# A row copy set behind other work, and two weight loads cut in halves, in a sparse attention and ELU MLP kernel

## The chip, the cores and the metric

The kernel runs on one core of one Trainium2 chip. The metric is device time in microseconds of one execution, smaller is better; where several runs were taken, their median counts. Five engines matter: TensorE (PE, matmuls; PEld is its weight loading), VectorE (DVE), ScalarE (ACT), GpSimd (POOL, which here issues the loads from HBM) and SyncE (SP, which issues the stores and the DMA transposes). Each works through its own list of instructions in order, and they wait for one another by semaphores.

## What is computed

Causal attention over 8 batches, 8 heads, 576 positions and 64 features per head, in which four heads see the last 32 positions ("local") and four see the earlier positions of the same remainder modulo 32 ("strided"); the heads of a token, side by side, are a row of `x`, which goes through two matmuls with an ELU between.

```python
rel = pos[:, None] - pos[None, :]
mask_local = (rel >= 0) & (rel < stride)
mask_strided = (rel >= 0) & (pos[None, :] % stride == pos[:, None] % stride)
...
attn = np.exp(scores)
attn = attn / (np.sum(attn, axis=-1, keepdims=True) + 1e-09)
return np.matmul(attn, v).astype(np.float32)
...
h = x @ w_in
g = np.where(h > 0.0, h, alpha * (np.exp(np.minimum(h, 0.0)) - 1.0))
return (g @ w_out).astype(np.float32)
```

`x` has 4608 rows of 512, `w_in` is 512 x 2048, `w_out` 2048 x 512. Inputs and output are float32; the kernel computes in bf16 with float32 sums.

## The kernel before

The order of all work is written out by hand, in the string `ORDER` (lines 35 to 145). Each word of it is one step; a loop at the end (lines 703 to 705) splits a word at its dots and calls the function of its first letter with the rest. Every engine gets its instructions in the order of these words, so a word's place counts against the words of the same engine and those it waits for.

The steps of attention, for a batch `b` and a pair of heads (`s` strided or `l` local, with y = 0 or 1; `0l1` is batch 0, local, y = 1) and half u:

- `D.what.b` issues loads on POOL (line 267). `D.vl` loads the rows of local v (line 260), `D.wi3.0` a quarter of `w_in` (512 columns, all four groups of 128 rows, line 275), `D.wo..` a quarter of `w_out`. Words with one number more (`D.kl.0.1`) load a part. Loads share eight semaphores in turn.
- `T` transposes q or k on PE (lines 404 to 415) and `c` (DVE) or `C` (ACT) copies the result. From batch 2 on, `X` does it by a DMA transpose on SP (line 604).
- `S.key.u.banks` computes scores into two PSUM banks (L456); `e` takes their exp on ACT (L463), into one of two buffers; `m` multiplies by the mask on DVE (L470 strided, L476 local).
- `O.key.u.banks` multiplies by ones, for the sums, and by v (L483 and L492 strided, L499 and L504 local in batches 0 and 1; L519 and L526 later); `n` takes the logarithm of the sums and `r` the exp of minus that, on ACT (L554, L559); `x` multiplies on DVE and writes a part of `xT` (L584).
- `V.b` copies, on DVE, the last 32 rows of each block of local v to the first rows of the next block (L588). The load of v must have landed, and L504 reads what V wrote. In batches 0 and 1 only; later a load does it (L262). `W` copies strided v (L591).
- `F.mk` makes the local mask on POOL (two selects, L349 and L352), `F.ml` spreads it on DVE (L357, L359).

The steps of the MLP, for a chunk of 512 tokens and a tile m of 128 of the 2048 columns:

- `a` does the first two of four matmuls of a tile, over the strided heads' features (row groups 2 and 3 of `w_in`), `b` the other two (groups 0 and 1, the local heads); `L` does all four (L611). The last number is the PSUM bank.
- `h` takes the exp (ACT, L619); `i` on DVE (L628) or `j` on ACT (L626) clamps it; `g` takes the maximum with h on DVE (L637, L639) and so frees the bank.
- `Z` does a quarter of the second matmul (L645), `o` (ACT) or `q` (DVE) copies the result (L651), `t` stores it (L663).

`w.bank.n...` are matmuls on zeros (L390) of n columns each, whose results are not used; they keep PE going at the start. Buffers come from small pools (two for e, five for masked scores, three for logarithms, line 169 on).

For `D.wi`, the function for loads already takes a third number: without one it loads all four row groups, with 0 the groups 2 and 3, with 1 the groups 0 and 1 (line 274).

Of the kernel before, what the change touches and what calls it, by code (L numbers as in the profile page):

```python
# [15 lines left out]
S = 576  # L16
# [30 lines left out]
h.0.15 b.0.12 h.0.14 i.0.15 b.0.0 h.0.12 b.0.13 i.0.14 g.0.15 h.0.0 a.0.3.7 D.vs.1 a.0.11.3 j.0.12
g.0.14 a.0.2.1 h.0.1 i.0.0 b.0.2 g.0.12 b.0.3 h.0.2 g.0.0 b.0.11 h.0.3 a.0.8.6 i.0.2 D.ql.1 h.0.11 i.0.1
a.0.6.4 g.0.2 h.0.13 a.0.5.0 b.0.8 g.0.1 a.0.4.1 D.kl.1 h.0.8 i.0.3 b.0.4 g.0.3 b.0.5 h.0.4 T.1s1.q.2
a.0.7.7 j.0.13 i.0.4 b.0.6 C.1s1.q g.0.4 b.0.7 D.vl.1 h.0.5 g.0.13 Z.0.1.0.2 h.0.6 i.0.5 Z.0.0.0.5 g.0.5  # L50
h.0.7 D.qs.2 j.0.6 i.0.8 a.0.9.1 i.0.7 a.0.10.0 g.0.8 b.0.9 g.0.6 j.0.11 b.0.10 g.0.7 h.0.9 T.1s1.k.6
Z.0.3.0.4 D.ks.2 h.0.10 g.0.11 j.0.10 Z.0.3.1.4 i.0.9 c.1s1.k g.0.10 Z.0.0.1.5 g.0.9 Z.0.1.1.2 D.kl.2
T.1s0.q.3 T.1s0.k.7 C.1s0.q Z.0.1.2.2 c.1s0.k S.1s0.1.01 S.1s1.0.67 Z.0.0.2.5 e.1s1.0 e.1s0.1 Z.0.0.3.5
m.1s0.1 m.1s1.0 S.1s1.1.01 S.1s0.0.67 e.1s1.1 Z.0.1.3.2 e.1s0.0 m.1s1.1 O.1s0.1.31 o.0.1 m.1s0.0
O.1s1.0.07 T.1l1.q.6 n.1s0.1 n.1s1.0 Z.0.3.2.4 c.1l1.q r.1s0.1 q.0.0 D.vs.2 r.1s1.0 O.1s1.1.76 x.1s1.0
T.1l1.k.5 n.1s1.1 O.1s0.0.21 c.1l1.k T.1l0.q.0 n.1s0.0 T.1l0.k.6 x.1s0.1 D.ql.2 Z.0.3.3.4 C.1l0.k
c.1l0.q r.1s1.1 V.1 S.1l0.1.01 r.1s0.0 S.1l0.0.56 x.1s1.1 Z.0.2.0.3 e.1l0.0 q.0.3 X.qs.2 e.1l0.1 m.1l0.0
S.1l1.1.56 e.1l1.1 m.1l0.1 S.1l1.0.01 O.1l0.0.74 e.1l1.0 X.ks.2 m.1l1.1 O.1l0.1.65 x.1s0.0 Z.0.2.1.3
n.1l0.0 n.1l0.1 m.1l1.0 r.1l0.0 O.1l1.1.54 t.0.3 r.1l0.1 x.1l0.0 O.1l1.0.21 n.1l1.1 x.1l0.1 Z.0.2.2.3
n.1l1.0 r.1l1.1 t.0.0 r.1l1.0 Z.0.2.3.3 x.1l1.1 x.1l1.0 X.kl.2 W.2 L.1.12.7 L.1.1.6 h.1.12 i.1.12  # L60
L.1.6.5 h.1.1 g.1.12 o.0.2 D.qs.3 L.1.0.4 i.1.1 h.1.6 g.1.1 L.1.4.7 h.1.0 i.1.6 g.1.6 L.1.5.6 X.ql.2
h.1.4 D.ks.3 i.1.0 j.1.4 L.1.3.5 g.1.0 D.vs.3 h.1.5 t.0.1 g.1.4 L.1.2.4 D.vl.2 h.1.3 i.1.5 i.1.3
S.2s1.0.01 S.2s1.1.23 h.1.2 g.1.3 L.1.10.7 e.2s1.0 g.1.5 D.ql.3 e.2s1.1 L.1.15.5 i.1.2 h.1.10 g.1.2
L.1.7.6 h.1.15 m.2s1.1 i.1.15 S.2s0.0.01 S.2s0.1.23 h.1.7 X.qs.3 g.1.15 L.1.13.4 e.2s0.1 i.1.10 j.1.7
L.1.9.5 m.2s0.1 g.1.10 L.1.8.3 g.1.7 h.1.9 e.2s0.0 i.1.9 L.1.14.7 X.ks.3 h.1.13 g.1.9 L.1.11.6 h.1.8
i.1.13 h.1.14 i.1.8 Z.1.2.0.5 t.0.2 g.1.13 h.1.11 j.1.14 g.1.8 O.2s1.1.01 Z.1.3.0.4 j.1.11 D.kl.4
n.2s1.1 g.1.11 Z.1.2.1.5 g.1.14 r.2s1.1 O.2s0.1.23 m.2s1.0 Z.1.3.1.4 n.2s0.1 x.2s1.1 O.2s1.0.67 r.2s0.1
Z.1.2.2.5 n.2s1.0 x.2s0.1 Z.1.3.2.4 r.2s1.0 m.2s0.0 O.2s0.0.01 x.2s1.0 Z.1.3.3.4 n.2s0.0 r.2s0.0
S.2l0.0.23 S.2l0.1.67 Z.1.2.3.5 o.1.3 x.2s0.0 e.2l0.1 Z.1.0.0.4 W.3 o.1.2 m.2l0.1 e.2l0.0 S.2l1.0.01
S.2l1.1.67 Z.1.1.0.5 e.2l1.1 m.2l0.0 e.2l1.0 m.2l1.1 O.2l0.0.23 D.kl.3 Z.1.0.1.4 n.2l0.0 m.2l1.0  # L70
O.2l1.1.01 r.2l0.0 O.2l1.0.67 Z.1.1.1.5 n.2l1.0 x.2l0.0 n.2l1.1 Z.1.1.2.5 r.2l1.0 O.2l0.1.23 Z.1.0.2.4
r.2l1.1 x.2l1.0 D.vs.4 n.2l0.1 x.2l1.1 Z.1.0.3.4 r.2l0.1 D.ks.4 Z.1.1.3.5 x.2l0.1 D.qs.4 S.3s0.0.01
S.3s0.1.67 q.1.1 L.2.5.3 e.3s0.0 D.vl.3 q.1.0 e.3s0.1 L.2.14.5 h.2.5 m.3s0.1 L.2.3.4 i.2.5 h.2.14 D.ql.4
g.2.5 X.kl.3 L.2.11.7 h.2.3 i.2.14 g.2.14 O.3s0.1.01 h.2.11 L.2.0.6 X.ql.3 i.2.3 m.3s0.0 n.3s0.1 L.2.4.5
i.2.11 r.3s0.1 g.2.3 t.1.3 O.3s0.0.23 h.2.0 g.2.11 L.2.8.4 h.2.4 x.3s0.1 L.2.2.7 n.3s0.0 i.2.4 X.qs.4
i.2.0 h.2.8 L.2.9.1 g.2.4 r.3s0.0 i.2.8 L.2.7.5 g.2.0 h.2.9 X.ks.4 h.2.2 g.2.8 L.2.10.0 h.2.7 i.2.2
x.3s0.0 L.2.13.6 X.kl.4 j.2.7 j.2.9 g.2.2 L.2.6.4 h.2.13 g.2.7 t.1.0 L.2.1.7 j.2.13 g.2.9 h.2.6 g.2.13
L.2.15.5 t.1.2 h.2.1 i.2.6 j.2.1 L.2.12.6 g.2.6 h.2.15 g.2.1 S.3s1.0.12 S.3s1.1.34 h.2.10 i.2.15
Z.2.1.0.7 e.3s1.1 i.2.10 e.3s1.0 m.3s1.1 Z.2.1.1.7 g.2.10 h.2.12 m.3s1.0 Z.2.0.0.4 i.2.12 g.2.15
S.3l0.0.01 S.3l0.1.23 g.2.12 Z.2.0.1.4 e.3l0.1 e.3l0.0 X.ql.4 m.3l0.1 S.3l1.0.23 S.3l1.1.56 Z.2.1.2.7  # L80
m.3l0.0 e.3l1.0 e.3l1.1 m.3l1.0 t.1.1 O.3s1.1.01 Z.2.1.3.7 n.3s1.1 m.3l1.1 O.3l1.1.23 r.3s1.1 O.3s1.0.56
Z.2.0.2.4 n.3l1.1 x.3s1.1 n.3s1.0 Z.2.0.3.4 q.2.1 r.3l1.1 O.3l1.0.01 t.2.1 r.3s1.0 Z.2.3.0.7 x.3l1.1
n.3l1.0 x.3s1.0 Z.2.3.1.7 r.3l1.0 S.4s1.0.23 S.4s1.1.56 x.3l1.0 Z.2.3.2.7 e.4s1.0 e.4s1.1 W.4 O.3l0.0.01
Z.2.3.3.7 q.2.0 n.3l0.0 D.vs.5 O.3l0.1.23 r.3l0.0 t.2.0 D.kl.5 Z.2.2.0.6 n.3l0.1 x.3l0.0 Z.2.2.1.6
r.3l0.1 m.4s1.1 O.4s1.1.01 x.3l0.1 Z.2.2.2.6 n.4s1.1 q.2.3 D.qs.5 L.3.2.5 r.4s1.1 m.4s1.0 D.ks.5 x.4s1.1
L.3.11.7 h.3.2 D.vl.4 i.3.2 S.4l0.0.01 S.4l0.1.23 h.3.11 g.3.2 L.3.14.4 e.4l0.1 i.3.11 e.4l0.0 L.3.7.5
m.4l0.1 g.3.11 S.4s0.0.01 S.4s0.1.23 m.4l0.0 h.3.7 Z.2.2.3.6 e.4s0.1 i.3.7 e.4s0.0 g.3.7 L.3.4.7 h.3.14
m.4s0.1 L.3.5.5 h.3.4 i.3.14 m.4s0.0 O.4s0.1.01 g.3.14 h.3.5 L.3.8.3 n.4s0.1 i.3.5 L.3.0.4 g.3.5 r.4s0.1
i.3.4 L.3.1.2 o.2.2 X.ks.5 x.4s0.1 h.3.0 O.4s0.0.56 g.3.4 h.3.8 L.3.3.1 i.3.0 X.qs.5 n.4s0.0 i.3.8
L.3.6.7 g.3.0 r.4s0.0 g.3.8 L.3.12.0 h.3.1 t.2.3 h.3.6 i.3.1 L.3.9.4 g.3.1 j.3.6 X.kl.5 L.3.10.3 h.3.3  # L90
x.4s0.0 h.3.9 i.3.3 L.3.15.2 h.3.12 g.3.3 h.3.10 D.ks.6 O.4l0.1.56 g.3.6 L.3.13.1 n.4l0.1 D.ql.5 i.3.12
g.3.12 Z.3.0.0.7 j.3.10 r.4l0.1 i.3.9 Z.3.2.0.0 g.3.10 h.3.13 g.3.9 h.3.15 Z.3.2.1.0 x.4l0.1 j.3.15
Z.3.0.1.7 D.qs.6 i.3.13 g.3.15 D.vl.5 O.4l0.0.34 g.3.13 Z.3.0.2.7 n.4l0.0 r.4l0.0 S.5s0.0.12 S.5s0.1.56
Z.3.0.3.7 e.5s0.0 x.4l0.0 e.5s0.1 Z.3.2.2.0 m.5s0.0 q.3.0 O.4s1.0.12 m.5s0.1 S.4l1.0.34 S.4l1.1.56
n.4s1.0 W.5 Z.3.1.0.7 e.4l1.1 Z.3.2.3.0 e.4l1.0 m.4l1.1 r.4s1.0 m.4l1.0 O.4l1.1.34 Z.3.1.1.7 X.ql.5
n.4l1.1 x.4s1.0 O.4l1.0.56 r.4l1.1 Z.3.1.2.7 X.ks.6 n.4l1.0 x.4l1.1 O.5s0.0.12 Z.3.1.3.7 r.4l1.0 X.qs.6
n.5s0.0 x.4l1.0 Z.3.3.0.4 r.5s0.0 O.5s0.1.56 L.4.3.3 n.5s0.1 x.5s0.0 Z.3.3.1.4 r.5s0.1 o.3.2 x.5s0.1
L.4.13.2 h.4.3 t.3.2 q.3.1 L.4.1.6 h.4.13 t.3.0 j.4.3 i.4.13 L.4.2.7 h.4.1 g.4.3 D.ks.7 t.2.2 L.4.5.5
h.4.2 g.4.13 D.vs.6 i.4.1 Z.3.3.2.4 t.3.1 h.4.5 D.vl.6 g.4.1 j.4.2 S.5l0.0.01 S.5l0.1.23 i.4.5 L.4.0.6
e.5l0.1 e.5l0.0 L.4.4.3 D.ql.6 h.4.0 m.5l0.0 g.4.2 L.4.12.2 j.4.0 g.4.5 h.4.4 L.4.7.7 h.4.12 i.4.4 g.4.0  # L100
Z.3.3.3.4 j.4.12 h.4.7 g.4.12 L.4.14.6 o.3.3 m.5l0.1 g.4.4 t.3.3 D.qs.7 S.6s0.0.45 S.6s0.1.01 h.4.14
L.4.15.2 i.4.7 e.6s0.0 g.4.7 e.6s0.1 L.4.6.3 i.4.14 h.4.15 m.6s0.1 S.5l1.0.01 S.5l1.1.45 m.6s0.0
L.4.11.7 i.4.15 e.5l1.1 g.4.14 D.kl.6 e.5l1.0 O.5l0.0.45 m.5l1.1 L.4.8.6 h.4.6 m.5l1.0 g.4.15 n.5l0.0
L.4.9.1 i.4.6 r.5l0.0 g.4.6 L.4.10.2 h.4.8 x.5l0.0 h.4.11 Z.4.1.0.3 i.4.8 h.4.10 i.4.11 h.4.9 Z.4.0.0.0
g.4.8 j.4.9 g.4.11 O.5l1.1.45 Z.4.0.1.0 i.4.10 n.5l1.1 g.4.9 D.ql.7 O.5l1.0.67 r.5l1.1 g.4.10 Z.4.1.1.3
n.5l1.0 x.5l1.1 O.5l0.1.12 r.5l1.0 Z.4.1.2.3 n.5l0.1 x.5l1.0 Z.4.0.2.0 r.5l0.1 S.5s1.0.45 S.5s1.1.67
# [629 lines left out]
```

## Time and profile before

| | us |
|---|---|
| median of 3 runs | 305.9 (305.54 to 307.13) |
| the profiled execution | 306.4 |
| its span, first to last instruction | 304.7 |
| PE busy | 293.7 (96%) |
| PEld, DVE, ACT busy | 147.4, 224.9, 223.3 |
| POOL busy | 79.8 |
| granted TensorE clock | 1.00 |

The page cuts the span into 40 slices (7.6 us each) and gives busy tenths of each; a 9 is 90% or more:

```profile
PE   8989999999999999999999999999999999999995
PEld 4644455445544454445544554455444544444444
DVE  6669858897599978998689867966699367996020
ACT  2868568789979887996988898978997569642011
POOL 8823334093670007080556051000000000000000
```

PE is busy nearly everywhere. DVE and ACT are near full in single slices, such as the ninth (DVE, 61 to 69 us) and the tenth (ACT). What a change of order is worth is therefore read from single waits, and the time of the profiled execution, 306.4, has 1.7 us outside the span.

### The profile page before, as it was taken

What the parts mean: (1) busy time and instruction counts of PE and PEld (TensorE: products, weight loads), DVE (VectorE), ACT (ScalarE), POOL (GpSimd) and SP (SyncE); (2) the same over time, 40 slices, a digit from 0 to 9 for tenths busy, and PEclk for the clock granted to TensorE, in tenths of its full rate; (3) what the DMA queues carried; (4) which work ended last, traced back from release to release, by engine and by line L of the source; (5) the groups of instructions that cost most, each with busy time, mean ns of one, the idle gap of its engine ahead of it and who ended that gap; (6) DMA issues with size and microseconds to landing.
All of it is one profiled execution on the core that took longest, in us unless ns stands there. A gap on an engine that the chain in (4) does not pass through costs nothing.

```text
span 304.7 us, 6207 instructions
## 1 busy us (share of the span) xinstructions
PE 293.7 (96%) x2294; PEld 147.4 (48%) x2333; DVE 224.9 (74%) x442; ACT 223.3 (73%) x402; POOL 79.8 (26%) x111
## 2 busy tenths in 40 slices
PE   8989999999999999999999999999999999999995
PEld 4644455445544454445544554455444544444444
DVE  6669858897599978998689867966699367996020
ACT  2868568789979887996988898978997569642011
POOL 8823334093670007080556051000000000000000
PEclk9999999999999999999999999999999999999999
DMA  8999999999999959999899599711120110110143
GB/s 162 187 207 206 208 192 167 166 230 159 132 148 153 196 154 148 170 140 155 160 188 196 40 174 164 115 61 36 42 65 0 37 34 0 37 36 0 37 137 104
DMA packets 107357, 37.62 MB, mean 123 GB/s; under 512 B 89152, under 2 KB 102848, under 8 KB 107328
## 3 DMA queue, kind: packets, MB, share of 16 engines
q0 software_dynamic: 69728, 19.47, 63.4%
q1 hardware_dynamic: 36836, 16.93, 27.3%
q10 hardware_dynamic: 764, 0.84, 0.9%
q8 instruction: 18, 0.29, 0.4%
q14 instruction: 11, 0.09, 0.1%
HBM read 39.53 MB, written 9.44 MB: 161 GB/s over the span
## 4 chain that ended last, share of the span: by engine, by line
PE 75%; DMA 9%; DVE 5%; ACT 5%; issue 3%; POOL 2%; SPq 0%; ACTq 0%; DVEq 0%; POOLq 0%
PE ps L645 34%; PE ps L611 31%; DMA kTs<-ks 4%; PE ps L456 3%; DMA out_dram<-osb 3%; DMA vl<-in_v_dram 3%; PE ps L519 2%; DVE g L639 2%; PE ps L526 2%; DVE he L628 1%; ACT ln L554 1%; PE ps L675 1%; ACT ln L559 1%; ACT he L619 1%; ACT e L463 1%
## 5 line engine op out<-in xcount | busy, mean ns | idle before, releaser
L645 PE MATMUL ps<-w_out_sb,g 128*128 128x512 bf16 x541 | 130.7, 379 | 1.4 <-issue 0.6
L611 PE MATMUL ps<-xT,w_in_sb 128*128 128x512 bf16 x558 | 129.5, 379 | 1.5 <-issue 0.3
L619 ACT ACTIVATE he<-ps 128x512 f32<-128x512 f32 x144 | 80.4, 596 | 24.8 <-PE ps L611 23.7
L611 PEld LDWEIGHTS <-w_in_sb 128*128 128x128 bf16 x576 | 54.9, 98 | 64.3 <-issue 0.7
L645 PEld LDWEIGHTS <-g 128*128 128x128 bf16 x560 | 50.8, 98 | 54.4 <-issue 0.3
L639 DVE TENSOR_TENSOR g<-he,ps 128x512 bf16<-128x512 bf16 x103 | 68.3, 681 | 1.6
L584 DVE TENSOR_TENSOR xT<-ps,ln 64x576 bf16<-64x576 f32 (+1 forms) x64 | 42.6, 678 | 21.9 <-ACT ln L559 20.2
L628 DVE TENSOR_SCALAR he<-he 128x512 bf16<-128x512 f32 x103 | 44.4, 444 | 12.1 <-ACT he L619 11.5
L463 ACT ACTIVATE e<-ps 72x576 bf16<-72x576 f32 (+1 forms) x64 | 38.8, 647 | 11.3 <-PE ps L456 8.5
L554 ACT ACTIVATE ln<-ps 64x576 f32<-64x576 f32 (+1 forms) x64 | 36.3, 584 | 9.5 <-PE ps L519 5.3
L559 ACT ACTIVATE ln<-ln 64x576 f32<-64x576 f32 (+1 forms) x64 | 38.4, 621 | 1.3
L637 DVE SCALAR_TENSOR_TENSOR g<-he,ps 128x512 bf16<-128x512 bf16 x41 | 27.5, 680 | 5.1 <-ACT he L626 4.8
L626 ACT ACTIVATE he<-he 128x512 bf16<-128x512 f32 x41 | 25.4, 630 | 1.8 <-DVE g L639 1.1
L651 ACT COPY osb<-ps 128x512 f32<-128x512 f32 x17 | 9.9, 584 | 17.6 <-PE ps L645 10.6
L250 POOL DMA_DIRECT2D kl<-in_k_dram x24 | 17.5, 738 | 18.6 <-DMA vl<-in_v_dram 8.0
L651 DVE COPY osb<-ps 128x512 f32<-128x512 f32 x18 | 12.2, 684 | 13.5 <-PE ps L645 12.3
L243 POOL DMA_DIRECT2D ql<-in_q_dram x24 | 20.0, 837 | 3.3 <-DMA qs<-in_q_dram 1.9
L476 DVE TENSOR_TENSOR pm<-e,mask_l 128x576 bf16<-128x576 bf16 x32 | 14.2, 455 | 7.8 <-ACT e L463 6.8
L470 DVE TENSOR_TENSOR pm<-e,mask_s 72x576 bf16<-72x576 bf16 x32 | 14.2, 449 | 3.9 <-ACT e L463 3.5
L233 POOL DMA_DIRECT2D vs<-in_v_dram x8 | 5.2, 649 | 35.6 <-DVE vsp L591 34.6
L519 PEld LDWEIGHTS <-vsp 72*128 72x128 bf16 x192 | 9.3, 98 | 5.4 <-DVE pm L470 0.5
L233 POOL DMA_DIRECT2D ks<-in_k_dram x7 | 4.6, 664 | 27.6 <-DMA kTs<-ks 25.8
(89 smaller groups left out, 156.8 us busy)
## 6 DMA issues: line engine op xcount, KB each, us to landing
out_dram<-osb SPq DMA_DIRECT2D x29, 144.0 KB
vl<-in_v_dram POOLq DMA_DIRECT2D x8, 288.0 KB, 10.2
w_in_sb<-in_moe_w_in_dram POOLq DMA_DIRECT2D x4, 512.0 KB, 12.0
w_out_sb<-in_moe_w_out_dram POOLq DMA_DIRECT2D x4, 512.0 KB, 18.1
kl<-in_k_dram POOLq DMA_DIRECT2D x24, 72.0 KB, 7.5
ql<-in_q_dram POOLq DMA_DIRECT2D x24, 72.0 KB, 10.1
qs<-in_q_dram POOLq DMA_DIRECT2D x5, 320.0 KB, 8.5
ks<-in_k_dram POOLq DMA_DIRECT2D x5, 320.0 KB, 6.3
```

Source lines behind the costliest of these rows:

```text
L463: nc.scalar.activation(e[0:R], tiles.pop(("S", key, u))[0:R], ACT.Exp, scale=scale)
L554: nc.scalar.activation(t, s_ps, ACT.Ln)
L559: nc.scalar.activation(t, t, ACT.Exp, scale=-1.0)
L584: nc.vector.tensor_mul(dst, o_ps, rc)
L611: nc.tensor.matmul(tiles["h", ch, m], lhsT=w_in_sb[:, c, m * 128:(m + 1) * 128], rhs=xT[:, c, ch * CHUNK:(ch + 1) * CHUNK], start=(c == 2) ...
L619: nc.scalar.activation(e, tiles["h", i[0], i[1]], ACT.Exp)
L626: nc.scalar.activation(e1, e, ACT.Relu, bias=1.0, scale=-1.0)
L628: eng.tensor_scalar(e1, e, scalar1=1.0, scalar2=1.0, op0=ALU.min, op1=ALU.subtract)
L637: nc.vector.scalar_tensor_tensor(dst, e1, -1.0, h, op0=ALU.mult, op1=ALU.max)
L639: nc.vector.tensor_tensor(dst, e1, h, op=ALU.max)
L645: nc.tensor.matmul(ops, lhsT=g[ch % 2][:, m, kk * 128:(kk + 1) * 128], rhs=w_out_sb[:, m, :], start=(m == 0), stop=(m == MC - 1), skip_gro ...
L651: eng(o_sb, tiles.pop(("o", int(ch), int(kk))))
```

## The change

Only `ORDER` changes; the functions stay as they are. In it:

- `V.0` goes from before `m.0l1.1` to behind `m.0l1.1`, `m.0l1.0` and `x.0s1.0`.
- `D.wi3.0` and `D.wi0.0` become two loads each: `D.wi3.0.0` and `D.wi0.0.0` where the whole loads stood (row groups 2 and 3), then `D.wi3.0.1` and `D.wi0.0.1` (groups 0 and 1), ahead of `D.wi2.0`.
- Of the matmuls on zeros, `w.0.224.168` and `w.6.237` go, and `w.4.512` has 512 columns more.
- In batch 0's local heads, the y = 0 units change places (`O.0l0.0` ahead of `O.0l0.1`, and the steps n, r, x, m with them), and `e.0l0.1` comes sooner.
- `b.0.1` goes behind `b.0.12`.
- `S.2s1.0` and `S.2s1.1` go behind `L.1.10`.
- `x.4l0.1` goes behind `i.3.13`, `g.3.15` and `g.3.13`.

All other words keep their order; lines are only filled anew. The lines in which words move, cut to these:

```diff
-T.0s0.q.1.6 e.0s0.0 D.vl.0 c.0s0.q.1 w.2.512.512.512 T.0s1.q.7 T.0s1.k.6 D.wi3.0 c.0s1.q S.0s0.1.01
-C.0s1.k m.0s0.0 T.0l1.k.5 D.wi0.0 e.0s0.1 c.0l1.k w.2.403 S.0s1.1.67 S.0s1.0.23 e.0s1.1
-m.0s0.1 w.4.512.406 T.0l1.q.5 e.0s1.0 m.0s1.1 D.wi2.0 O.0s0.1.47 c.0l1.q O.0s1.1.61 n.0s0.1 m.0s1.0
-D.wi1.0 S.0l1.1.23 n.0s1.1 e.0l1.1 w.0.370 T.0l0.k.7 D.qs.1 O.0s0.0.51 r.0s1.1 O.0s1.0.03 F.mk r.0s0.1
-T.0l0.q.2 x.0s1.1 C.0l0.k x.0s0.1 D.wo0.0 c.0l0.q n.0s1.0 w.5.224.224.224.224.206 S.0l1.0.67 n.0s0.0
-F.ml S.0l0.1.23 e.0l1.0 D.ks.1 V.0 r.0s1.0 w.4.512.512 S.0l0.0.67 m.0l1.1 r.0s0.0 x.0s1.0 e.0l0.0
-w.4.512 O.0l1.1.41 m.0l1.0 n.0l1.1 x.0s0.0 w.0.224.168 O.0l1.0.07 e.0l0.1 D.wo1.0 w.6.237 a.0.15.1
-n.0l1.0 m.0l0.1 a.0.14.6 r.0l1.1 m.0l0.0 r.0l1.0 O.0l0.1.75 x.0l1.1 O.0l0.0.32 x.0l1.0 n.0l0.1 a.0.12.4
-n.0l0.0 a.0.13.5 r.0l0.1 r.0l0.0 D.wo2.0 a.0.1.2 x.0l0.1 x.0l0.0 a.0.0.0 b.0.1 D.wo3.0 b.0.15 b.0.14
-h.0.15 b.0.12 h.0.14 i.0.15 b.0.0 h.0.12 b.0.13 i.0.14 g.0.15 h.0.0 a.0.3.7 D.vs.1 a.0.11.3 j.0.12
+T.0s0.q.1.6 e.0s0.0 D.vl.0 c.0s0.q.1 w.2.512.512.512 T.0s1.q.7 T.0s1.k.6 D.wi3.0.0 c.0s1.q S.0s0.1.01
+C.0s1.k m.0s0.0 T.0l1.k.5 D.wi0.0.0 e.0s0.1 c.0l1.k w.2.403 S.0s1.1.67 S.0s1.0.23 e.0s1.1 m.0s0.1
+w.4.512.406 T.0l1.q.5 e.0s1.0 D.wi3.0.1 m.0s1.1 D.wi0.0.1 D.wi2.0 O.0s0.1.47 c.0l1.q O.0s1.1.61 n.0s0.1
+m.0s1.0 D.wi1.0 S.0l1.1.23 n.0s1.1 e.0l1.1 w.0.370 T.0l0.k.7 D.qs.1 O.0s0.0.51 r.0s1.1 O.0s1.0.03 F.mk
+r.0s0.1 T.0l0.q.2 x.0s1.1 C.0l0.k x.0s0.1 D.wo0.0 c.0l0.q n.0s1.0 w.5.224.224.224.224.206 S.0l1.0.67
+n.0s0.0 F.ml S.0l0.1.23 e.0l1.0 D.ks.1 r.0s1.0 w.4.512.512 S.0l0.0.67 m.0l1.1 r.0s0.0 m.0l1.0 x.0s1.0
+e.0l0.0 w.4.512.512 V.0 e.0l0.1 O.0l1.1.41 x.0s0.0 n.0l1.1 O.0l1.0.07 m.0l0.0 D.wo1.0 n.0l1.0 a.0.15.1
+a.0.14.6 m.0l0.1 r.0l1.1 O.0l0.0.32 r.0l1.0 O.0l0.1.75 x.0l1.1 x.0l1.0 n.0l0.0 n.0l0.1 a.0.12.4 a.0.13.5
+r.0l0.0 r.0l0.1 D.wo2.0 a.0.1.2 x.0l0.0 x.0l0.1 a.0.0.0 D.wo3.0 b.0.15 b.0.14 h.0.15 b.0.12 h.0.14
+i.0.15 b.0.1 b.0.0 h.0.12 b.0.13 i.0.14 g.0.15 h.0.0 a.0.3.7 D.vs.1 a.0.11.3 j.0.12 g.0.14 a.0.2.1 h.0.1
...
-h.1.4 D.ks.3 i.1.0 j.1.4 L.1.3.5 g.1.0 D.vs.3 h.1.5 t.0.1 g.1.4 L.1.2.4 D.vl.2 h.1.3 i.1.5 i.1.3
-S.2s1.0.01 S.2s1.1.23 h.1.2 g.1.3 L.1.10.7 e.2s1.0 g.1.5 D.ql.3 e.2s1.1 L.1.15.5 i.1.2 h.1.10 g.1.2
+L.1.3.5 g.1.0 D.vs.3 h.1.5 t.0.1 g.1.4 L.1.2.4 D.vl.2 h.1.3 i.1.5 i.1.3 h.1.2 g.1.3 L.1.10.7 S.2s1.0.01
+S.2s1.1.23 e.2s1.0 g.1.5 D.ql.3 e.2s1.1 L.1.15.5 i.1.2 h.1.10 g.1.2 L.1.7.6 h.1.15 m.2s1.1 i.1.15
...
-g.3.12 Z.3.0.0.7 j.3.10 r.4l0.1 i.3.9 Z.3.2.0.0 g.3.10 h.3.13 g.3.9 h.3.15 Z.3.2.1.0 x.4l0.1 j.3.15
-Z.3.0.1.7 D.qs.6 i.3.13 g.3.15 D.vl.5 O.4l0.0.34 g.3.13 Z.3.0.2.7 n.4l0.0 r.4l0.0 S.5s0.0.12 S.5s0.1.56
+j.3.10 r.4l0.1 i.3.9 Z.3.2.0.0 g.3.10 h.3.13 g.3.9 h.3.15 Z.3.2.1.0 j.3.15 Z.3.0.1.7 D.qs.6 i.3.13
+g.3.15 D.vl.5 O.4l0.0.34 g.3.13 x.4l0.1 Z.3.0.2.7 n.4l0.0 r.4l0.0 S.5s0.0.12 S.5s0.1.56 Z.3.0.3.7
```

## The prediction

> **What bounds the kernel now.** I read the shares of busy time first, then what TensorE (PE) waits for, then the timelines around those waits. From the page's first part and PE's list of waits (us in total, times, longest):
>
> ```profile
> PE 293.7 (96%) x2294; PEld 147.4 (48%) x2333; DVE 224.9 (74%) x442; ACT 223.3 (73%) x402; POOL 79.8 (26%) x111
> ...
> PE ps L499 <- DVE pm L476: 1.1, 1, 1.1
> ...
> PE ps L456 <- DVE g L639: 0.5, 1, 0.5
> PE ps L456 <- DMA kTs<-ks: 0.5, 1, 0.5
> ```
>
> PE works through 96% of the span, so this change can only give back places where PE stands still. Three count, and each is touched by a part of the change: L499 (local attention of batch 0), L456 behind the DMA transpose of batch 2's strided keys, and L456 behind an ELU result. Counted in issue slots (0.216 us is the step between starts of 512-column matmuls of L611) PE is free there for 1.24 us (from 14.94+0.22 to 16.40), 0.65 us (60.24+0.22 to 61.10) and 0.66 us (138.74+0.22 to 139.61).
>
> **Part 1: V.0 behind two masks and one x; the split loads; three warm-up groups less.** The timelines of POOL and DVE around it:
>
> ```profile
> 6.45 0.61 POOL L233 DMA_DIRECT2D ql<-in_q_dram  x1
> 7.07 1.18 POOL L260 DMA_DIRECT2D vl<-in_v_dram  x1
> 8.24 3.00 POOL L275 DMA_DIRECT2D w_in_sb<-in_moe_w_in_dram  x4
> 11.30 0.65 POOL L233 DMA_DIRECT2D xT<-in_q_dram  x1
> 11.96 0.34 POOL L349 TENSOR_SCALAR_AFFINE_SELECT mask<-mask 128x96 bf16<-128x96 bf16 x1
> 12.37 0.32 POOL L352 TENSOR_SCALAR_AFFINE_SELECT mask<-mask 128x96 bf16<-128x96 bf16 x1
> ...
> 15.57 0.75 POOL L279 DMA_DIRECT2D w_out_sb<-in_moe_w_out_dram  x1 [1.53 <-DMA vl<-in_v_dram]
> 17.73 0.74 POOL L279 DMA_DIRECT2D w_out_sb<-in_moe_w_out_dram  x1 [1.42 <-DMA w_in_sb<-in_moe_w_in_dram]
> ```
>
> ```profile
> 14.16 0.10 DVE L359 MEMSET mask_l<- 32x48 uint32 x1
> 15.31 0.55 DVE L588 COPY vl<-vl 32x1472 bf16<-32x1472 bf16 x1 [1.05 <-DMA vl<-in_v_dram]
> 15.89 0.46 DVE L476 TENSOR_TENSOR pm<-e,mask_l 128x576 bf16<-128x576 bf16 x1
> ```
>
> DVE stands 1.05 us for the load of v (landed 15.28), then copies its rows (0.55), and only then masks; PE's L499 needs both and starts at 16.40. Moved ahead, the two masks and the x (0.37 us a step: 15.89, 16.26, 16.63) would fill the wait, and V.0 could end near 15.9.
>
> But the split has a price on POOL's queue. POOL's later loads wait for the load eight before them: the w_out load at 15.57 waited for vl, eight loads earlier, the next for the first w_in; each starts 0.28 us after that landing (15.28 to 15.57, 17.45 to 17.73). Two more w_in loads move D.qs.1 from eight behind the second vs load (landed 11.02, issue 11.30) to eight behind the second ql load, which was issued at 6.45 and landed 6.12 later, at 12.57. So D.qs.1 goes out at about 12.57+0.28 = 12.85, and F.mk, queued behind it, ends 1.38 after that (11.30 to 12.68 now): 14.23, not 12.68. F.ml on DVE, now 13.77 to 14.25, waits for it: 14.3 to 14.8. Issuing itself is not the limit: 512 KB take 0.75, 320 KB 0.65, so the four halves cost 4 x 0.65 - 2 x 0.75 = 1.1 us more of POOL, inside the same wait.
>
> Then on DVE: masks 14.8 and 15.2 (their exps ended 12.3 and 14.65), the x at 15.55 (its reciprocal 14.98), V.0 15.95 to 16.5, covered data since 15.28. L499 starts at 16.53, 0.13 us later than now. Given back behind it: the second local unit follows at once, since its mask is done at 15.6 and not 17.08; ACT's next two exps, which wait for the two e buffers, run at 15.36 and 15.98 instead of 16.44 and 17.28; the logarithm of the first sums ends at 17.3 (now 17.39), so L611 starts at 17.35 (now 17.62). Two tiles of it, two local units, 0.36 + 0.28 + 0.86: the next L611 at 18.94 (now 19.22), its second tile held by the last logarithm to 19.45, the third at 19.88 instead of 20.09. Part 1 is **-0.2 us** at the start of the dense L611 stretch. Bounds: -0.5 if F.mk is not held, +0.3 if its two selects take twice 0.33 beside DVE work. The warm-ups fall by 629 columns and rise by 512; they fill waits, and PE's idle stretch (15.37 to 16.53, now 15.16 to 16.40, with the granted clock at 1.00 through it) grows no longer: nothing. The batch-0 units of y = 0 that change places, and b.0.1 behind b.0.12, wait for nothing either.
>
> The halves: L611's only wait for w_in is 0.3 us at 20.04 (third tile, w_in landed 20.00). Half one of that quarter lands about 1.25 us after the first quarter's half instead, near 17.7, and both second halves by 20.0, before the first b at 20.75. Later landings stay: POOL's starts behind w_in and xT landings are 17.73, 20.28, 23.00, 25.50, 27.10, i.e. 2.55, 2.72, 2.50 us per 512 KB and 1.60 per 320 KB, 0.005 us per KB both ways, with no fixed part over 0.1 us per load. The w_out loads and D.ks.1 go out up to 3 us later behind the same eight-load wait, into a queue that is full either way; the first w_out quarter lands at 29.35 and is used at 30.7. So nothing.
>
> The Trainium skill, "DMA: Bandwidth & Descriptors", section "Anatomy of one DMA — SWDGE (gpsimd) path": a load costs a fixed 2.0 us beside its bytes, so cutting loads up is dear. These rows deny that for loads in a full queue; were it serial, two loads more would put all later landings 4 us back (an estimate from that page), and the sum near 309.5.
>
> **Part 2: S.2s1 one L tile later.** Timelines of PE, ACT and DVE:
>
> ```profile
> 61.10 0.43 PE L456 MATMUL ps<-qTs,kTs 64*128 64x72 bf16 x16 [0.48 <-DMA kTs<-ks]
> 61.47 2.76 PE L611 MATMUL ps<-xT,w_in_sb 128*128 128x512 bf16 x12
> 61.45 1.19 ACT L463 ACTIVATE e<-ps 72x576 bf16<-72x576 f32 x2 [0.20 <-PE ps L456]
> 63.41 0.60 ACT L619 ACTIVATE he<-ps 128x512 f32<-128x512 f32 x1 [0.21 <-PE ps L611]
> 64.04 0.43 DVE L628 TENSOR_SCALAR he<-he 128x512 bf16<-128x512 f32 x1 [0.45 <-ACT he L619]
> ```
>
> The keys' transpose lands at 61.06; it hangs on loads that land in a queue kept full (206 GB/s from 15 to 45 us), not on PE. So what part 1 gave is waited away here, unless work is put in front. That is done: L.1.10.7 (4 x 0.216 = 0.86) runs from 60.26 (60.46 less 0.2) to 61.12; its bank is free since g.1.4 ended, 60.14. S.2s1 starts at 61.14, as now, with 0.86 us of PE work done ahead. PE can't keep all of it: ACT's queue still has its two exps at 61.48 and h.1.10 at 62.64; h.1.15 follows at 63.13 instead of 63.41, DVE's clamp at 63.76 instead of 64.04, its g.1.15 ends 64.91 instead of 65.19, and that frees the bank of L.1.9.5, at 64.97. Now that tile starts at 65.40. **-0.43 us**; behind it the same steps follow one another, as now. Bounds: -0.2 (part 1 gave nothing, so S.2s1 starts 0.2 late) and -0.85 (0.65 + 0.2, all kept).
>
> **Part 3: x.4l0.1 three DVE operations later.**
>
> ```profile
> 137.29 0.74 DVE L584 TENSOR_TENSOR xT<-ps,ln 64x576 bf16<-64x576 f32 x1
> 137.96 0.41 DVE L628 TENSOR_SCALAR he<-he 128x512 bf16<-128x512 f32 x1
> 138.29 0.67 DVE L637 SCALAR_TENSOR_TENSOR g<-he,ps 128x512 bf16<-128x512 bf16 x1
> 138.89 0.67 DVE L639 TENSOR_TENSOR g<-he,ps 128x512 bf16<-128x512 bf16 x1
> ```
>
> The last g ends at 139.56 and frees the bank of S.5s0.0. Without the x before it (0.67 a step) it ends at 138.89; S.5s0.0 goes at 138.95. But S.5s0.1 takes banks 5 and 6, where x.4l0.1 reads; x now ends at 139.56, so S.5s0.1 starts at 139.61 instead of behind S.5s0.0 at 139.79. Only S.5s0.0's 8 matmuls are won: **-0.17 us** (bounds 0 and -0.66).
>
> **Sum.** Part 1's 0.2 is not added: before the transpose it only lets L.1.10.7 start in time. So -0.43 - 0.17 = -0.6 us. No later use of a transposed tile comes within 4.7 us of its landing, so the shift reaches the end. The profiled execution took 306.4, 1.7 more than its span of 304.7: span 304.1, execution 305.8. It lies 0.5 above the median of the runs, 305.9; on that, **305.3**.
>
> **Rivals.**
> Nothing is carried: ACT and DVE, busy 1.51 and 1.97 of the 2 us from 60 to 62, hold PE again at once; 305.9. For it: DVE's share. Against it: ACT's three waits for L611 just behind.
> All three stalls vanish: -0.2 - 0.65 - 0.66 = -1.5, 304.4. For it: PE is the bound elsewhere; against: the banks above.
> The transpose lands 2 us later, as it shares the DMA engines with the ql loads and stores of 48 to 56 us: it took 12.24 us from issue to landing, that of the queries just before 8.64; 2 us is about half that spread. It decides from a landing at 61.12 on, where L.1.10.7 ends: +2.0 - 0.6 = +1.4, 307.3. Against it: neither transposes nor their neighbours are reordered.
> Slower by the split: each load more holds the queue for a fixed time c, all landings behind come 2c late, batch 2's transpose too; beyond 2c = 0.6 the gain is gone. The farthest row is v's load, 288 KB in 2.71 us (12.57 to 15.28) against 1.44 by the KB: c = 1.3, +2.6 - 0.4, 308.1. Against it: its pieces are small, those of the halves are not. The Trainium skill's section named above has the same rule, with its larger figure.
>
> **Chances.** Forecast 0.54, nothing carried 0.14, all stalls 0.16, late transpose 0.10, fixed cost 0.06. A measurement of this kernel can't tell under 0.5% (1.5 us: 304.4 to 307.4) from no change. Faster: half of "all stalls" and a tenth of the forecast, 0.13. Slower: the fixed cost and some 0.06 of late transposes, 0.12. Same: 0.75. Range 304.2 to 307.0: it leaves out the fixed cost, half the late transposes, and some of "all stalls", under 0.2.
>
> **What would show it.** F.mk's selects near 13.5 to 14.2 and F.ml at 14.3 (wrong if still 13.8); V.0 without a wait, L499 near 16.5; the third tile of L611 at 19.9; PE without the 0.5 us wait for kTs, L.1.9.5 0.4 us earlier; at 139 S.5s0.1 held by x. The forecast is wrong if the transpose lands later than 61.1 or w_in is waited for.

## The result, and the profile after

The changed kernel takes 306.62 us (median of 22 runs), the kernel before 305.59 beside it (22 runs): a ratio of 1.0037, 95% interval 1.0025 to 1.005. It was forecast 0.6 us faster and is 1.0 us slower. By the 0.5% that counts here as a difference it is no change, but the sign is wrong and the interval leaves no doubt of it. Six of the changed kernel's 22 executions took 307.4 us or more, as did three of twelve when eight idle instructions were added to it further down, against 2 of all 121 executions of the kernel before; none of these nine was profiled, so what they lost is open.

The profiled execution after took 306.09 us with a span of 304.4, again 1.7 apart. The kernel before has one with a span of 304.7, which took 0.8 more than the median of that kernel's runs here, so the two spans can't be compared with each other as they stand; their parts can. The start first: POOL, DVE and PE in the timelines of the changed kernel (start, duration, engine, line and operation; in brackets the idle time ahead of it and what ended it; "..." stands for rows left out).

```profile
10.67 2.40 POOL L275 DMA_DIRECT2D w_in_sb<-in_moe_w_in_dram  x3 [0.33 <-DMA ql<-in_q_dram]
13.17 0.65 POOL L233 DMA_DIRECT2D xT<-in_q_dram  x1
13.82 0.33 POOL L349 TENSOR_SCALAR_AFFINE_SELECT mask<-mask 128x96 bf16<-128x96 bf16 x1
14.22 0.31 POOL L352 TENSOR_SCALAR_AFFINE_SELECT mask<-mask 128x96 bf16<-128x96 bf16 x1
```

```profile
14.89 0.10 DVE L359 MEMSET mask_l<- 32x48 uint32 x1
14.98 0.83 DVE L476 TENSOR_TENSOR pm<-e,mask_l 128x576 bf16<-128x576 bf16 x2
15.73 0.45 DVE L584 TENSOR_TENSOR xT<-ps,ln 128x288 bf16<-128x288 f32 x1
16.21 0.55 DVE L588 COPY vl<-vl 32x1472 bf16<-32x1472 bf16 x1
```

```profile
15.70 0.31 PE L499 MATMUL ps<-pm,ones 128*64 128x288 bf16 x2
16.81 0.32 PE L504 MATMUL ps<-pm,vl 128*64 128x96 bf16 x6 [0.80 <-DVE vl L588]
...
17.39 1.02 PE L611 MATMUL ps<-xT,w_in_sb 128*128 128x512 bf16 x4
...
61.72 0.43 PE L456 MATMUL ps<-qTs,kTs 64*128 64x72 bf16 x16
...
65.66 3.61 PE L611 MATMUL ps<-xT,w_in_sb 128*128 128x512 bf16 x16 [0.34 <-DVE g L639]
```

The start went as forecast: D.qs.1 goes out late, F.mk stands behind it, the masks come before V.0, V.0 waits for nothing, and L611 starts at 17.39 (17.35 was forecast, 17.62 before). At 61 us PE no longer waits for the transposed keys (line 456); four tiles later it waits 0.34 us for an ELU result instead, and L.1.9.5, which began at 65.40 before, begins at 65.66.

So far nothing costs 1 us. The last piece of PE's work in the chain of work that ends last (start, duration), before and after, shows where it is:

```profile
297.50 3.55 PE ps L675 x48
```

```profile
296.34 3.55 PE ps L675 x48
```

In these two executions the last matmul ends at 301.05 before and at 299.89 after, 1.16 us *earlier*; yet the span is only 0.3 shorter. From the last matmul to the end of the span it is 3.62 us before and 4.50 after. In that stretch there are only two evictions and the last stores. The DMA queues from there on, 301.2 to 304.6 us before and 300.1 to 304.3 after (queue, kind: packets, MB, share of 16 engines):

```profile
q1 hardware_dynamic: 244, 0.13, 15.1%
q10 hardware_dynamic: 160, 0.07, 7.3%
```

```profile
q1 hardware_dynamic: 240, 0.13, 12.3%
q10 hardware_dynamic: 160, 0.07, 5.9%
q14 instruction: 1, 0.01, 0.9%
```

These are the same stores (240 and not 244 packets, as the second stretch begins a little later behind the last matmul), and one packet more: a fetch of instructions, 8192 bytes, at 301.4 us, taking 0.62. Before, the fetch that answers to it came at 304.9, when all was over. The last store is delivered in 16 parts by 16 DMA engines; when SP issued it and when each part was done, in order, from the trace's DMA events (us):

```
before  issued 301.53: 303.28 303.30 303.30 ... 303.41 303.43 303.46
after   issued 300.38: 302.12 302.13 302.13 ... 302.29 302.29 303.17
```

Fifteen engines are done 1.9 us after the issue in both; in the changed kernel the sixteenth is 0.88 late, and the kernel ends with it.

Whose instructions are these? The trace records 577 instructions on DVE before, semaphore instructions among them, and at five of its fetches DVE had done or begun 64, 198, 318, 447 and 577 of them: a block of 8192 bytes per some 128. (Of the other fetches of this size five fit ACT's count in the same way: 68, 194, 323, 447, 576.) In the changed kernel there are 578. The one more lies at the reordered masks: m.0l1.0 now stands straight behind F.ml and m.0l1.1 and has to wait for DVE and for ACT (its exp) both, and a semaphore instruction of its own (at 15.03 us, line 476) takes one of the two waits. So each later instruction of DVE lies one place further on. The counts are only a rough guide: the fetch that came at 223.3 us with 447 instructions done came at 216.0 with 438 in the changed kernel, and one place does not account for that. By the times, the fetch at 304.9 was asked for by the semaphore instruction behind DVE's DRAIN (303.84, 1.1 us ahead), and the one at 301.4 by that DRAIN itself (ended 300.26, 1.1 us ahead). Both are the 575th recorded instruction of DVE. That is a reading so far; the experiments test it.

### The profile page after: what moved, and what is told of

It reads as the page before. It is cut to its first block, busy times and chain, and to the rows that moved or that the text cites. A ratio compares the mean times of both kernels' runs of the same rounds, so it can differ in the third digit from the quotient of the medians.

```text
span 304.4 us, 6245 instructions
## 1 busy us (share of the span) xinstructions
PE 296.2 (97%) x2331; PEld 146.5 (48%) x2331; DVE 224.4 (74%) x442; ACT 223.3 (73%) x402; POOL 81.4 (27%) x113
## 4 chain that ended last, share of the span: by engine, by line
PE 87%; DVE 4%; ACT 2%; DMA 2%; issue 1%; POOL 1%; ACTq 0%; POOLq 0%; DVEq 0%
PE ps L645 39%; PE ps L611 37%; PE ps L456 3%; PE ps L526 2%; PE ps L519 2%; DMA ql<-in_q_dram 2%; DVE g L639 1%; PE ps L675 1%; DVE he L628 1%; ACT he L619 1%; PE ps L413 1%; DVE xT L584 0%; ACT e L463 0%; PE ps L390 0%; ACT ln L554 0%
## 5 line engine op out<-in xcount | busy, mean ns | idle before, releaser
L645 PE MATMUL ps<-w_out_sb,g 128*128 128x512 bf16 x560 | 133.4, 379 | 0.1
L611 PE MATMUL ps<-xT,w_in_sb 128*128 128x512 bf16 x576 | 131.3, 379 | 0.4 <-DVE g L639 0.3
L619 ACT ACTIVATE he<-ps 128x512 f32<-128x512 f32 x144 | 80.3, 596 | 25.5 <-PE ps L611 23.8
L611 PEld LDWEIGHTS <-w_in_sb 128*128 128x128 bf16 x576 | 54.8, 98 | 64.7 <-issue 1.5
```

The lines of the kernel that those rows point to most:

```text
L611: nc.tensor.matmul(tiles["h", ch, m], lhsT=w_in_sb[:, c, m * 128:(m + 1) * 128], rhs=xT[:, c, ch * CHUNK:(ch + 1) * CHUNK], start=(c == 2) ...
L619: nc.scalar.activation(e, tiles["h", i[0], i[1]], ACT.Exp)
L645: nc.tensor.matmul(ops, lhsT=g[ch % 2][:, m, kk * 128:(kk + 1) * 128], rhs=w_out_sb[:, m, :], start=(m == 0), stop=(m == MC - 1), skip_gro ...
```

## The experiments

### One part of the change at a time

Four kernels, each with one part: the halves alone, the reordered start alone (whole w_in loads), S.2s1 alone, x.4l0.1 alone.

```diff
-T.0s0.q.1.6 e.0s0.0 D.vl.0 c.0s0.q.1 w.2.512.512.512 T.0s1.q.7 T.0s1.k.6 D.wi3.0 c.0s1.q S.0s0.1.01
-C.0s1.k m.0s0.0 T.0l1.k.5 D.wi0.0 e.0s0.1
+T.0s0.q.1.6 e.0s0.0 D.vl.0 c.0s0.q.1 w.2.512.512.512 T.0s1.q.7 T.0s1.k.6 D.wi3.0.0 c.0s1.q S.0s0.1.01
+C.0s1.k m.0s0.0 T.0l1.k.5 D.wi0.0.0 e.0s0.1
...
-e.0s1.0 m.0s1.1 D.wi2.0
+e.0s1.0 D.wi3.0.1 m.0s1.1 D.wi0.0.1 D.wi2.0
```

> The kernel before with only the four half loads of w_in in place of two whole ones; V.0 and all else stay. Theory 'split': the two loads more make all later landings late (0.8 us later in the one profile of the changed kernel: the two w_in quarters' last landings 25.99 against 25.22, batch 1's v 40.94 against 40.42), so this part alone takes the whole loss: ratio 1.003 or more (+1 us). Rival 'transpose first': the loss lies in S.2s1 behind L.1.10, so this alone gives 1.000 within 0.001. Rival 'start': the loss lies in V.0 and its neighbours, 1.000 here too.

Measured: 305.89 us, ratio 1.0006 (0.9986 to 1.0027). Last matmul to end 3.63 us.

```diff
-D.ks.1 V.0 r.0s1.0 w.4.512.512 S.0l0.0.67 m.0l1.1 r.0s0.0 x.0s1.0 e.0l0.0
-w.4.512 O.0l1.1.41 m.0l1.0
+D.ks.1 r.0s1.0 w.4.512.512 S.0l0.0.67 m.0l1.1 r.0s0.0 m.0l1.0 x.0s1.0 e.0l0.0
+w.4.512.512 V.0 e.0l0.1 O.0l1.1.41
...
```

> The kernel before with only the start reordered: V.0 behind two masks and one x, the zero matmuls, the y = 0 units and b.0.1 as in the changed kernel; w_in in whole loads. Theory 'split': no loss, 0.998 to 1.000, with L499 near 16.0 since the masks are not held up. Rival 'start': 1.002 or more. Rival 'transpose first': 1.000 within 0.001, as what is won is waited away before batch 2's scores.

Measured: 306.69 us, ratio 1.0027 (1.0009 to 1.0045). Last matmul to end 4.34 us, with a fetch at 301.7.

```diff
-S.2s1.0.01 S.2s1.1.23 h.1.2 g.1.3 L.1.10.7
+h.1.2 g.1.3 L.1.10.7 S.2s1.0.01 S.2s1.1.23
```

> The kernel before with only S.2s1 behind L.1.10. Theory 'split': faster, 0.998 to 0.999, by the 0.43 us of the prediction. Rival 'transpose first': the two exps of S.2s1 come up to 0.6 us later (62.1 for 61.45 in the profile of the changed kernel) and hold ACT and DVE: 1.002 or more.

Measured: 305.52 us, ratio 1.0001 (0.9982 to 1.0021). Last matmul to end 3.63 us.

```diff
-Z.3.2.1.0 x.4l0.1 j.3.15
+Z.3.2.1.0 j.3.15
...
-g.3.13 Z.3.0.2.7
+g.3.13 x.4l0.1 Z.3.0.2.7
```

> The kernel before with only x.4l0.1 behind three operations of DVE. All theories: 0.998 to 1.000 by the 0.17 us of the prediction (0.55 us in the one profile of the changed kernel). If this part had the loss, 1.002 or more, by a wait behind 140 us that the profile does not show.

Measured: 305.82 us, ratio 0.9997 (0.9979 to 1.0015). Last matmul to end 3.62 us.

What follows: the loss is in the reordered start. No price of the halves and no gain of the two later moves is seen; the intervals, some 0.6 us to either side, would hide a small one. So the theory that the halves take the whole loss is out. In its profile the start alone is not slower at the start (PE is 0.27 us ahead of the kernel before at the third tile of L611). Of the four it alone has, like the changed kernel, 578 instructions on DVE. That can be tested without the start.

### One instruction more on DVE, and eight

Into the kernel before: one small memset of a tile that nothing reads any more, in an idle stretch of DVE near 283 us.

```diff
-Z.7.2.3.6 Z.7.0.3.4 q.7.2
+Z.7.2.3.6 Z.7.0.3.4 k.1 q.7.2
...
+        "k": lambda n: [nc.vector.memset(eq, 0.0) for _ in range(int(n))],
```

> The kernel before, order untouched, with one small memset more on DVE (of a tile that nothing reads any more) in an idle stretch near 285 us, so one instruction more in DVE's stream (578, as in the changed kernel and in the one with the start alone; 577 before). Theory 'fetch in the tail': the block of DVE's instructions that was fetched when all was over (304.9 us) is now fetched 1.1 us after DVE's DRAIN, among the last stores; one DMA engine delivers its part of the last stores late: last matmul to end of span 4.3 to 4.5 us, not 3.62; ratio 1.002 to 1.004. Rival 'the reordered start costs something in most executions which one profile does not show': tail 3.6, ratio 0.999 to 1.001.

Measured: 306.64 us, ratio 1.0024 (1.001 to 1.0037); last matmul to end 4.46 us. The queues in the last 4.2 us of its span:

```profile
q1 hardware_dynamic: 244, 0.13, 12.3%
...
q14 instruction: 1, 0.01, 0.9%
```

The fetch is there, at 303.0 for 0.63 us, 1.1 us behind the DRAIN (ended 301.92); the last store (issued 302.03) is done on 15 engines at 303.97 and on the sixteenth at 304.79. An instruction of 0.09 us in an idle stretch costs 0.7 us at the end (0.3 to 1.1 by the interval).

With eight (k.8 in the place of k.1; 584 instructions):

> The same with eight memsets (a net seven or eight instructions more on DVE). Theory 'fetch in the tail': the block is now asked for by an instruction near 293 us, is there before the last stores are issued, and the tail is 3.6 again; ratio 0.999 to 1.001: more instructions, less time than with one. Rival 'any instruction added near the end costs': slower than with one memset, over 1.003. Rival 'the start': 0.999 to 1.001, as for one.

Measured: 305.78 us, ratio 1.0003 (0.9991 to 1.0014); last matmul to end 3.55 us; the fetch came at 296.7. More instructions, less time: it is not the instruction that costs, but where in the kernel the block boundary falls. In all 14 profiles the fetch shows 1.1 to 1.2 us behind the 575th recorded instruction of DVE (behind its end, in this kernel behind its start); what changes is whether that instruction comes ahead of the last stores, among them or behind them.

The changed kernel with the same k.8 (585 instructions):

> The changed kernel with the same eight memsets. Theory 'fetch in the tail': tail 3.6, not 4.50, so 0.9 us of the 1.03 lost come back: ratio 0.998 to 1.001. Rival 'the start': as the changed kernel, 1.003 to 1.005.

Measured: 305.72 us against 305.62, ratio 1.0019 with a wide interval (0.9991 to 1.0047), which by itself doesn't decide; last matmul to end 3.52 us, the fetch at 296.5. The profile shows the mechanism; of the time only the median shows it.

### One instruction less, by one swap

The changed kernel, and then the reordered start alone, with x.0s1.0 ahead of m.0l1.0. Behind the x, m.0l1.0 needs no second wait: 577 instructions again.

```diff
-S.0l0.0.67 m.0l1.1 r.0s0.0 m.0l1.0 x.0s1.0
+S.0l0.0.67 m.0l1.1 r.0s0.0 x.0s1.0 m.0l1.0
```

> The changed kernel with x.0s1.0 ahead of m.0l1.0 instead of behind it; the mask then no longer waits for DVE and ACT both, which takes one semaphore instruction from DVE's stream (577 again). Theory 'fetch in the tail': the fetch is at the end of the span again, tail 3.6, ratio 0.998 to 1.001, though all of the change but one order of neighbours is in it. Rival 'the start': 1.003 to 1.005, since V.0 is still behind two masks and one x.

> The reordered start alone, whole w_in loads, with x.0s1.0 ahead of m.0l1.0, so that DVE has 577 instructions and not 578. Against the start alone (ratio 1.0027, tail 4.34) it differs in that one swap. Theory 'fetch in the tail': tail 3.6, ratio 0.9985 to 1.0005. Rival 'V.0 behind the masks is what costs': still 1.002 or more.

Measured: the changed kernel with the swap 305.48 us, ratio 0.9996 (0.9982 to 1.001), last matmul to end 3.62; the start alone with it 305.59, ratio 0.9999 (0.9983 to 1.0015), 3.64. In both the fetch came 0.2 us or more behind the span's end, and in the first of them the last store's sixteenth engine is done 0.03 us behind the fifteenth. The first keeps all of the change but the order of one pair of neighbours, and the loss is gone. Eleven kernels without a fetch in the last stretch have 3.52 to 3.64 us from the last matmul to the end, three with one 4.34 to 4.50.

### What the halves cost, and what the moves give

All four quarters of w_in in two loads each, in the kernel before:

```diff
...
-D.wi2.0
+D.wi2.0.0 D.wi2.0.1
...
-D.wi1.0
+D.wi1.0.0 D.wi1.0.1
```

> The kernel before with all four w_in quarters in two loads each, four loads more. Theory 'each load more costs the queue about 0.2 us that shows from the load of v (strided) on': that load lands near 41.2 (40.0 to 40.6 with none, 40.6 to 40.9 with two loads more), the keys' transpose of batch 2 near 61.9, S.2s1 starts 0.8 us later than before; ratio 1.001 to 1.003. Rival 'the 0.4 us of the halved kernels are scatter between runs': 40.0 to 40.6 and 60.9 to 61.5.

Measured: 310.89 us, ratio 1.0176 (1.014 to 1.0211), far more than either theory said, and by another way. The later loads are not later: the load of strided v that landed at 40.42 before lands at 40.30, and the keys' transpose at 60.42 (61.06 before). So the 0.4 us by which those landings had been late in the halved kernels does not grow with the number of loads, and is hardly a price of a load; this rests on one profile. The time is lost between 15 and 19 us (POOL's timeline, then one of PE's waits: total, times, longest):

```profile
15.48 0.71 POOL L275 DMA_DIRECT2D w_in_sb<-in_moe_w_in_dram  x1 [2.18 <-DMA vl<-in_v_dram]
...
17.07 0.33 POOL L349 TENSOR_SCALAR_AFFINE_SELECT mask<-mask 128x96 bf16<-128x96 bf16 x1
```

```profile
PE ps L499 <- DVE pm L476: 4.1, 1, 4.1
```

The last half waits for the load eight before it, that of local v (landed 15.20), and F.mk stands behind it: the selects are 3.2 us later than in the changed kernel, with its two loads more. PE idles 4.1 us, and then its clock is low. In the table of stretches (us of the stretch, its length, busy and instructions of PE, weight loads, DVE, ACT and POOL, then the granted clock, the DMA engines' share and GB/s) of this kernel:

```profile
19.00:22.00 3.00, 2.61 (x21) 1.50 (x21) 2.48 (x7) 2.48 (x6) 1.64 (x3) 0.50 1.24 206
22.00:26.00 4.00, 4.00 (x25) 1.75 (x24) 1.43 (x4) 1.57 (x5) 2.29 (x4) 0.56 1.24 205
```

The clock is 0.50 and 0.56 where the kernel before has 1.00 (from 14 to 19 us it was still 0.97 here); PE is 5.0 us behind the kernel before at the tile that there began at 19.2 us, and 6.15 at 30.5.

The other way round, the changed kernel with whole loads and the swap:

```diff
-D.wi3.0.0
+D.wi3.0
...
-m.0l1.0 x.0s1.0
+x.0s1.0 m.0l1.0
```

> The changed kernel with whole w_in loads (no halves) and the swap: reordered start, S.2s1 one tile later, x.4l0.1 later, no fetch in the tail. Theory 'the halves made the later loads land 0.4 us later and so took what S.2s1's move gave': the keys' transpose of batch 2 lands near 61.1 (61.4 to 61.8 with halves), PE's L.1.9.5 starts 0.4 or more earlier than before, ratio 0.997 to 0.999. Rival 'the moves give nothing that lasts': 0.9995 to 1.0005.

Measured: 305.6 us against 305.5, ratio 0.9997 (0.9982 to 1.0012); the transpose landed at 61.23, L.1.9.5 started 0.6 us later than before. With these two runs little speaks for the theory that the halves had taken what S.2s1's move gave, though the interval still reaches into the 0.997 to 0.999 that it forecast. In this execution the load of local v landed at 15.89 (15.28 before), all behind it followed, and PE waited 1.0 us for a whole w_in quarter. No profile with halves shows such a wait; that the halves would save it when v is late is likely, not tested.

Both later moves in the kernel before:

```diff
-S.2s1.0.01 S.2s1.1.23 h.1.2 g.1.3 L.1.10.7
+h.1.2 g.1.3 L.1.10.7 S.2s1.0.01 S.2s1.1.23
...
-g.3.13 Z.3.0.2.7
+g.3.13 x.4l0.1 Z.3.0.2.7
```

> The kernel before with both later moves (S.2s1 behind L.1.10.7, x.4l0.1 behind g.3.13), its start as before. Theory 'each move gives what its place shows' (0.4 and 0.2 us): ratio 0.998. Rival 'nothing that lasts' (each alone measured 1.0001 and 0.9997): 0.9995 to 1.0005. Tail 3.6 by both.

Measured: 305.51 us against 305.5, ratio 0.9995 (0.9975 to 1.0016). PE's timeline of it:

```profile
61.19 0.43 PE L456 MATMUL ps<-qTs,kTs 64*128 64x72 bf16 x16
...
65.28 3.61 PE L611 MATMUL ps<-xT,w_in_sb 128*128 128x512 bf16 x16 [0.49 <-DVE g L639]
```

The wait for the transpose is gone (0.48 us) and stands four tiles later, for g, at 0.49: L.1.9.5 starts at 65.28, 0.12 earlier than before. The clamp ahead of that g, 0.43 us in the kernel before, takes 0.79 here; beside it the row of POOL that it begins in:

```profile
63.71 0.79 DVE L628 TENSOR_SCALAR he<-he 128x512 bf16<-128x512 f32 x1 [0.38 <-ACT he L619]
```

```profile
63.07 1.18 POOL L260 DMA_DIRECT2D vl<-in_v_dram  x1
```

The clamp ends 0.25 us behind POOL's issue of the load. That is no accident of this profile: of the 1442 clamps on DVE in the 14 profiles, 101 took over 0.5 us, and each of these began while POOL was issuing a load and ended 0.22 to 0.26 us behind the end of that issue. Not every clamp that begins during an issue is held, and no run tests it by moving a load.

One execution says little here, since kernels with the very same order up to 280 us differ by up to 0.8 us at its end. From 13 profiles (the kernel with four quarters in halves is left out), how much longer (+) or shorter (-) PE took for three stretches, in us, than in the profile of the kernel before, as a mean over the kernels without and with the part that bears on it (how many, in brackets):

```
stretch (first to last instruction)           without the part   with it
0 to the third tile of L611 (20.31)            +0.03 (7)         -0.25 (3: start and halves)
                                                                 +0.06 (3: start, whole loads)
first scores of batch 1 to Z.1.2.0.5 (68.65)   +0.11 (7)         +0.24 (6: S.2s1 moved)
119.22 to the first L of chunk 4 (148.63)      -0.26 (7)         -0.51 (6: x.4l0.1 moved)
```

Single values lie up to 0.8 from these means, so the first and third gains are possible, not shown, and of the second the means show nothing. None of the twelve kernels is faster than the kernel before by more than its interval; with the swap the change is harmless, as fast as the kernel before within 0.2%.

## Why the prediction was wrong

**The step that failed** is the sum's "so the shift reaches the end": that whatever PE saves comes off the time, with all behind the last matmul taken as it was. That stretch grew by 0.88 us, since a fetch of DVE's instructions fell among the last stores. The prediction counted operations and loads, and no semaphore instructions; it never asked where in each engine's stream the blocks end. No rival had this either. Of the loss of 1.03 us by the medians, one instruction more on DVE gives 0.7 (0.3 to 1.1) by itself in the kernel before, and taking it away gives all of it back (0.9996 with the swap): shown.

That turned the sign. The gain of 0.6 did not come either: with the swap, and so without the fetch, the change measures 0.9996 (0.9982 to 1.001), from 0.55 us faster to 0.3 slower. That lies with the sum's largest term, Part 2 below. That the time still falls inside the range, 304.2 to 307.0, is luck: its upper end stood for a late transpose, and that is not what came.

**Part 1, the start: right, by its steps.** D.qs.1 at 13.17 (12.85 forecast; the load it waits for landed 0.3 later than before), the selects at 13.82 and 14.22, F.ml at its end 14.99 (14.3 to 14.8), V.0 without a wait, PE 0.20 ahead at the third tile (0.2 forecast). Wrong was which instruction PE waits at: L499 goes at 15.70, as the masks alone suffice for it, and L504 behind it stands 0.80 us for V.0. The price is the same, as L611 comes behind both (17.39; 17.35 forecast).

**The halves: nothing seen, as forecast** (1.0006, by the interval 0.4 us faster to 0.8 slower), and the eight-load wait that the prediction read off POOL's rows is real and steep. With two loads more F.mk still comes in time; with four the kernel takes 5.4 us longer. The prediction named the mechanism, and not that there is an edge.

**Part 2, S.2s1: a term of -0.43, of which the means above show nothing.** (The times alone, 0.6 us to either side, can't tell 0.43 from nothing.) In the profile of the move alone the step was right: S.2s1 started at 61.28, its g ended at 64.96 (64.91 was forecast) and L.1.9.5 started at 65.01. But with S.2s1 behind L.1.10.7 the score's exps, the next exp, the clamp and g follow in one row from whenever S.2s1 starts, and PE waits for that row at L.1.9.5. In all six kernels with the move L.1.9.5 starts 3.30 us plus the clamp's time behind S.2s1. Both terms were taken as fixed, and neither was: S.2s1 came between 61.19 and 62.07, by landings and PE's own delays (61.14 was forecast), and the clamp took 0.43 to 0.95 us (0.43 only in the kernel in which no issue of POOL held it). "The same steps follow one another" held for their order and not for their times. This is the rival "nothing is carried", for this part, and its place was the one that the rival named: DVE and ACT hold PE again.

**Part 3, x.4l0.1: -0.17 forecast,** -0.25 between the means above; that lies within their scatter, so it is no proof of the term.

**The rivals that fell.** A fixed cost per load (308.1): with two loads more the ratio is 1.0006, and four loads more don't move later landings. The Trainium skill, "DMA: Bandwidth & Descriptors", section "Anatomy of one DMA — SWDGE (gpsimd) path", gives 2.0 us fixed per load, and puts most of it down to the wait for completion and not to the setup; in a queue that is kept full no run here shows any of it. A transpose 2 us late (307.3): it landed at 61.36 after, 61.06 before. That is later than the 61.1 which the prediction named as a sign against itself, but S.2s1 started at 61.72 and did not wait for it. The time came out near 306.6 by neither.

## What to carry to other kernels

When a kernel's trace shows all its work earlier and its end not, look at what lies between the last matmul and the end, store by store, and at instruction fetches among the DMA queues; a neighbour swap that changes the number of semaphore instructions can move one into that stretch or out of it. Test a suspected shift of that kind by adding one, then several, idle instructions to the kernel before: a cost that appears with one and goes with eight is one of position. And a stall taken away by putting work in front of it is only won if the chain that begins behind the stall is not itself what PE waits for next; read that chain's links in several profiles before taking their times as fixed.

## What the runs showed of the hardware

A fetch of an engine's instructions shares the DMA engines with the kernel's own stores: 8192 bytes for 0.62 us on the queue of kind "instruction" put one of the sixteen parts of the last store 0.88 us back. The kernel before has eleven more such fetches ahead of its end (at 23.8, 32.2, 66.5 us and so on); what they cost, no run here tests. The Trainium skill, "Runtime: NRT & Kernel Launch", section "Instruction fetch mechanics", says of a block boundary: "The cost of crossing a 16 KiB boundary is one DMA tail-bump, mostly hidden." For the last one in the changed kernel "hidden" does not hold. The blocks differ too: DVE's are 8 KiB here, one per some 128 instructions (the 18 packets of 16384 bytes fit PE's 4648 recorded instructions, 256 each). DVE had only its closing instructions left then; what the fetch put back is not DVE's work but the store that the DMA engines were to deliver.

In the kernel with four quarters in halves the granted clock was 0.50 from 19 to 22 us, after PE had stood 4.1 us, from 15.3 to 19.4 us, and still 0.56 on average from 22 to 26 us, though PE was busy all that time; the stall of 4.1 us put PE 6.15 back.

In the 14 profiles a clamp on DVE (line 628) that took over 0.5 us and not some 0.43 had, 101 times out of 101, begun while POOL was issuing a load, and ended 0.22 to 0.26 us behind that issue.
